# One index search over four key sets, with a second pass of the program kept as a fallback

## The chip, the cores and the metric

The kernel runs on one core of a Trainium2 chip. A core has five engines that follow their own instruction queues: PE (matrix products), DVE (vector work along the rows of 128 partitions), ACT (functions and scaled copies), POOL (here it issues the gathers) and SP (here it issues plain loads and stores). Results of PE lie in PSUM, all other tiles in SBUF. The metric is the device time of one execution in microseconds (us); the median of several runs counts.

## The reference

The output is the sum of three terms for 2048 tokens of 448 channels: the input `x`, a long causal convolution (part A), and a product-key mixture of experts (part B). The change is in part B, on the layer-normed input:

```python
q = einsum("nd,dhc->nhc", xf, w_q)            # 16 heads, two halves of 256
s1 = einsum("nhd,ed->nhe", q[..., :256], k1)  # 64 keys a half
s2 = einsum("nhd,ed->nhe", q[..., 256:], k2)
i1 = argsort(-s1)[..., :2]; t1 = the scores there     # the same for s2: i2, t2
cand = t1[..., :, None] + t2[..., None, :]            # 4 candidates
eidx = i1[..., :, None] * 64 + i2[..., None, :]
top_s, top_e = the best 2 of the 4 candidates, and their eidx
g = softmax(top_s)
act = gelu(einsum("nd,nhkd->nhk", xf, u[top_e]))
out = einsum("nhk,nhk,nhkd->nd", g, act, v[top_e])
```

So for each token, head and half, the two best of 64 scores are needed with their places; 32 such key sets a token. Two experts a head are 32 rows of `u` and `v` a token, fetched from HBM. Part A is a shift convolution, a product, a convolution of length 2048 by Fourier transforms, and a gate.

## The kernel before, in words

The 2048 tokens are 16 tiles T of 128 tokens. Three stages follow each other; within a stage the queues of all engines are filled by a planner.

**Weights.** `w_load` brings the query weights head by head, `w_keys` (L315) multiplies them by the keys on PE, `w_out` (L323) copies the product from PSUM on ACT, `w_turn` transposes it, and `w_high` and `w_low` (L339 to L347) split it into a high and a low part. The score of a key is then one product of a token with a column of 448 entries.

**Scores.** For each tile, `s_turn` (L359 to L364) transposes the tokens, `s_split` splits them, and `s_mm` (L375 to L379) makes 4 groups of 512 scores in one PSUM bank each: 8 key sets of 64 (4 heads of 2 halves), 11 products a group. `s_top` then works on DVE: for each set one MAX8 (L419), which writes the 8 largest of 64 scores, and one `max_index` (L417), which writes their 8 places. A `max_index` is two instructions, MATCH_VALUE_LOAD (the 8 values) and FIND_INDEX8 (the pass over the scores). `s_pairs` (L438 to L466) takes the first two values and places of each set for a pair of tiles, forms the candidates, their order and the expert numbers; `s_gate` forms the softmax of two on ACT; `s_place` (L498) and `s_put` (L481, L482) bring expert numbers and gates to the layout of the gathers, with ACT copies into `idx` (integers) and `gt`.

**Experts.** They run beside the scores and the convolution. `e_gather` (L520) issues 512 indirect DMAs from POOL, each with 128 rows of 3.5 KB; four make a block in one of four buffers `uv` (128 blocks in all). Per block, `e_dots` multiplies the `u` half by the tokens on DVE (L552 for several rows at once, L559 for one with its sum), `e_gelu` sums on ACT (L571) and takes the gelu (L575), `e_weigh` multiplies by the gates (L586) and, after the scores stage, spreads the weights on DVE (L591; `e_scale` does it on ACT, L601, in the scores stage), and `e_values` multiplies the `v` half on PE (L611, L614), which frees the buffer. `e_spread` (L533) copies tokens to the rows that need them, `e_fold` (L633, L635) adds the result to the output.

**Convolution.** It begins when the score buffers are freed: loads of `hkv` (L651), taps (L661 to L680), transforms (L705, L733, L765), products (L750 to L756), the way back (L781, L801) and the gate (L810, L815), in two halves of channels. The stores (L640) come last.

**The order.** Each function yields operations with an engine, a cost, what they wait for and which buffers they take. The planner keeps a clock per engine and picks, each time, the operation that could start first, or one of a lower priority number (`PRIO`) that starts soon enough. `HOP` is the time it allows for a wait across engines, `LATE` how long after the expected landing of a gather its product is placed, `BEHIND` how a gather is ordered behind PE instructions, `AHEAD` how far the convolution may run ahead of the gathers. In the scores stage, gathers come first while fewer than `LEAD` numbered gathers lie ready. The order is fixed when the kernel is built; an engine never departs from it.

Of the kernel before, what the change touches and what calls it, by code (L numbers as in the profile page):

```python
# [10 lines left out]
F32 = mybir.dt.float32  # L11
# [7 lines left out]
P = 128  # L19
# [8 lines left out]
BEHIND = 0.2  # L28
PAD = 1.0
LEAD = 12  # L30
SPAN, AHEAD, WORK = 25.0, -0.010, 548.0
# [47 lines left out]
PRIO = {"c_back": 0.5, "c_delta": -0.1, "c_fin": -0.1, "c_fm": -0.4, "c_gate": -0.1, "c_hh": 0.4, "c_in": 0.5, "c_inv": 0.2, "c_load": -0.4, "c_mul": -0.2, "c_prod": 0.1, "c_spec": 0.3, "c_store": 0.2, "c_tap": 0.5, "c_turn": 0.4, "c_zt": 0.3, "e_dots": 0.2, "e_fold": -0.3, "e_gather": -0.2, "e_gelu": -0.2, "e_out": -0.1, "e_scale": -0.3, "e_spots": -0.2, "e_spread": -0.5, "e_values": -0.5, "s_gate": 0.1, "s_put": -0.5, "s_split": 0.1, "s_top": 0.3, "s_turn": 0.1}  # L79
# [18 lines left out]
class Planner:  # L98
# [3 lines left out]
    HOP, SLIP, RATE = 0.70, 1.20, 0.35  # L102
# [89 lines left out]
def parallel_kernel(ctx, tc, x, wq, kk, uv, hkv, const, fq, out):  # L192
    nc = tc.nc
    ctx.enter_context(tc.manual_schedule())
    ap = ctx.enter_context(tc.tile_pool(name="ap", bufs=1))
# [36 lines left out]
    xls = [wp.tile([P, KC + 1, P], F32R, name=f"xl{i}") for i in range(2)]  # L232
    live = {}
# [165 lines left out]
    def s_top(groups):  # L399
        for group in groups:  # L400
            n_t = len(group)
            def begin(n_t=n_t):
                live["mx"] = wp.tile([P, 2, 32, 8], F32, tag="mx", name="mx")
                live["mi"] = wp.tile([P, 2, 32, 8], U32, tag="mi", name="mi")

            for i, T in enumerate(group):
                for n in range(4):
                    for what in range(2):
                        for j0 in range(0, 8, 2):
                            def top(i=i, T=T, n=n, j0=j0, what=what, begin=begin):  # L410
                                if T % 2 == n == j0 == what == 0:
                                    begin()
                                mx, mi, sc = live["mx"], live["mi"], live["sc", T, n]
                                for j in range(j0, j0 + 2):
                                    m = mx[:, T % 2, 8 * n + j, :]
                                    if what:
                                        nc.vector.max_index(mi[:, T % 2, 8 * n + j, :], m, sc[:, 64 * j:64 * j + 64])  # L417
# [495 lines left out]
```

## Time and profile before

| What | Value |
| --- | --- |
| Median of 3 runs | 825.22 us (823.52 to 825.5) |
| The profiled execution's own time | 829.65 us |
| Span of its profile | 827.8 us |
| Busy in the span: PE, DVE, ACT, POOL | 675.5, 695.4, 560.2, 492.6 us |
| FIND_INDEX8 of L417 | 512 of 225 ns on the mean |
| MATCH_VALUE_LOAD of L417 | 512 of 75 ns |
| MAX8 of L419 | 512 of 217 ns |
| Gathers of L520 | 512, 234.91 MB, 77.0% of the DMA engines' time |
| All DMA | 278.53 MB, 336 GB/s over the span |

The profile follows one execution. A group is all instructions of one line, engine and shape; "mean ns" is the length of one from start to end, and as an engine begins an instruction before the one ahead has ended, 512 times the mean can be more than the time that they take. "Idle before" is how long the engine stood still in front of the group's instructions, with what ended it. The chain of work that ended last is followed back from the last instruction. A table of stretches gives each engine's busy time in a window of the span, with the granted clock of PE, the busy share of the DMA engines and what they moved.

### The profile page before, as it was taken

The numbers are of one execution on the slowest core, as the hardware profiler recorded it, in microseconds if no ns is written. First come the engines' busy times: TensorE is split into PE (matmuls) and PEld (weight loads), VectorE is DVE, ScalarE is ACT, GpSimd is POOL, SyncE is SP. The second block draws the span as 40 slices with busy tenths as digits, with TensorE's granted clock in tenths as the row PEclk, the third lists the DMA queues.
The fourth block names the chain that finished last, engine by engine and source line by source line (L and its number), as shares of the span: only waits on it lengthen the run. The fifth ranks groups of instructions, "written<-read, shape, count | busy, mean of one in ns | idle before, by whom it ended". The sixth has DMA issues, their size and how long they took to land.

```text
span 827.8 us, 16797 instructions
## 1 busy us (share of the span) xinstructions
PE 675.5 (82%) x5052; PEld 392.6 (47%) x5052; DVE 695.4 (84%) x2600; ACT 560.2 (68%) x1926; POOL 492.6 (60%) x518
## 2 busy tenths in 40 slices
PE   6994799999999989846776879787867778878784
PEld 2463456566565556414543344335545543433461
DVE  3369698999999999964898999996859989999674
ACT  4458997677777768664785765766557857666752
POOL 0004666666666757764577666667564776777770
PEclk9998699999998999956987989999888999999897
DMA  9954898999988989999999899999999999999995
GB/s 331 381 210 171 304 337 312 324 338 335 326 316 312 339 286 344 353 341 377 363 320 322 307 400 331 399 340 371 379 383 322 332 378 396 385 399 378 347 379 191
DMA packets 80555, 278.53 MB, mean 336 GB/s; under 512 B 10321, under 2 KB 47569, under 8 KB 80465
## 3 DMA queue, kind: packets, MB, share of 16 engines
q0 software_dynamic: 40960, 234.91, 77.0%
q1 hardware_dynamic: 39360, 42.41, 15.2%
q8 instruction: 41, 0.67, 0.3%
q14 instruction: 50, 0.40, 0.1%
q10 hardware_dynamic: 144, 0.13, 0.1%
HBM read 273.75 MB, written 3.67 MB: 335 GB/s over the span
## 4 chain that ended last, share of the span: by engine, by line
DVE 49%; DMA 20%; PE 17%; ACT 5%; issue 4%; SPq 4%; POOL 1%; DVEq 0%; POOLq 0%; ACTq 0%
DVE uv L552 18%; DMA uv<-in_uv_dram,idx 12%; DVE mi L417 9%; DMA x<-in_hkv_dram 7%; DVE mx L419 6%; SPq L651 4%; PE pw L315 4%; ACT uv L571 3%; PE pv L614 2%; PE psu L765 2%; DVE tap L672 2%; DVE tap L670 2%; DVE hh L751 2%; DVE hh L750 2%; DVE hh L755 2%
## 5 line engine op out<-in xcount | busy, mean ns | idle before, releaser
L520 POOL DMA_INDIRECT uv<-in_uv_dram,idx x512 | 491.9, 961 | 315.7 <-issue 94.0
L571 ACT ACTIVATE uv<-uv 128x448 f32<-128x448 f32 x457 | 257.7, 565 | 108.7 <-DVE uv L552 106.7
L552 DVE TENSOR_TENSOR uv<-xr,uv 128x1792 f32<-128x1792 f32 (+3 forms) x128 | 232.4, 1817 | 34.1 <-DMA uv<-in_uv_dram,idx 29.6
L614 PE MATMUL pv<-uv,cc 128*32 128x448 f32 x1024 | 144.9, 606 | 0.0
L417 DVE FIND_INDEX8 mi<-mx,sc 128x8 uint32<-128x64 f32 x512 | 104.1, 225 | 0.0
L765 PE MATMUL psu<-hh,fm 128*128 128x224 f32 x264 | 69.4, 388 | 25.8 <-DVE hh L756 16.7
L571 ACT ACTIVATION_READ_ACCUMULATOR uv<-uv 128x1 f32 x457 | 85.6, 187 | 0.0
L375 PE MATMUL sc<-wh,xh 128*128 128x512 f32 x192 | 81.9, 426 | 4.2 <-DVE mi L417 2.7
L705 PE MATMUL ps<-cst,x 128*64 128x132 f32 x896 | 69.2, 315 | 18.7 <-DVE x L687 6.5
L765 PEld LDWEIGHTS psu<-hh,fm 128*128 128x128 f32 x264 | 48.0, 200 | 71.0 <-ACT uv L571 43.0
L705 PEld LDWEIGHTS ps<-cst,x 128*64 128x64 f32 x896 | 60.4, 158 | 41.6 <-issue 20.4
L419 DVE MAX8 mx<-sc 128x8 f32<-128x64 f32 x512 | 74.3, 217 | 5.3 <-PE sc L379 5.2
L377 PE MATMUL sc<-wh,xl 128*128 128x512 f32 x192 | 77.0, 401 | 0.0
L376 PE MATMUL sc<-wl,xh 128*128 128x512 f32 x192 | 76.8, 400 | 0.0
L733 PE MATMUL psf<-x,fm 128*128 128x448 f32 x132 | 64.3, 575 | 2.5 <-DMA fm<-in_fq_dram 0.7
L611 PE MATMUL pv<-uv,cc 128*1 128x4 bf16 x128 | 21.6, 169 | 51.9 <-DVE cc L591 41.2
L611 PEld LDWEIGHTS <-cc 128*1 128x1 bf16 x128 | 10.2, 80 | 107.4 <-DVE cc L591 64.3
L601 ACT ACTIVATE cc<-rep,w 128x32 f32<-128x32 f32 x200 | 47.4, 308 | 9.6 <-DVE w L586 9.6
L375 PEld LDWEIGHTS sc<-wh,xh 128*128 128x128 f32 x192 | 36.9, 192 | 35.3 <-issue 14.8
L533 PE MATMUL xr<-xn,rep 32*128 32x448 f32 x128 | 34.8, 620 | 13.8 <-DVE uv L552 10.7
L715 ACT ACTIVATE x<-ps 128x396 f32<-128x396 f32 (+1 forms) x84 | 35.4, 457 | 14.4 <-PE ps L705 14.4
L624 ACT ACTIVATE vs<-pv 128x448 f32<-128x448 f32 x64 | 34.1, 532 | 13.2 <-PE pv L614 12.9
(103 smaller groups left out, 1036.8 us busy)
## 6 DMA issues: line engine op xcount, KB each, us to landing
wq<-in_wq_dram SPq DMA_DIRECT2D x16, 896.0 KB
x<-in_hkv_dram SPq DMA_DIRECT2D x14, 780.0 KB
fm<-in_fq_dram SPq DMA_DIRECT2D x66, 128.0 KB
uv<-in_uv_dram,idx POOLq DMA_INDIRECT x512
out_dram<-acc SPq DMA_DIRECT2D x32, 112.0 KB
acc<-in_x_dram SPq DMA_DIRECT2D x1, 2240.0 KB
acc<-in_x_dram SPq DMA_DIRECT2D x1, 896.0 KB
cst<-in_const_dram SPq DMA_DIRECT2D x1, 540.0 KB
```

The source lines that it names most:

```text
L375: nc.tensor.matmul(sc, xh[:, c, :], wh[:, c, ns], start=(c == 0), stop=False)
L376: nc.tensor.matmul(sc, xh[:, c, :], wl[:, c, ns], start=False, stop=False)
L377: nc.tensor.matmul(sc, xl[:, c, :], wh[:, c, ns], start=False, stop=False)
L417: nc.vector.max_index(mi[:, T % 2, 8 * n + j, :], m, sc[:, 64 * j:64 * j + 64])
L419: nc.vector.max(m, sc[:, 64 * j:64 * j + 64])
L520: made = nc.gpsimd.indirect_dma_start(live["uv", b][:, c, :], None, uv, bass.IndirectOffsetOnAxis(ap=idx[:, T, g:g + 1], axis=0)).ins
L552: nc.vector.tensor_mul(u, live["xr", T, j][:, None, :D].broadcast_to([P, na, D]), u)
L571: nc.scalar.activation(u, u, AF.Copy, accum_out=live["act", b][:, c:c + 1])
L614: nc.tensor.matmul(pv[32 * c:32 * c + 32, :D], cc[:, c, :], buf[:, c, D:], start=(hf == 0), stop=(hf == 1), tile_position=(0, 32 * c))
L705: nc.tensor.matmul(ps[64 * i:64 * i + 64, w * j:w * j + w], src, f1[:, i, :], start=True, stop=True, tile_position=(0, 64 * i))
L733: nc.tensor.matmul(ps[:, :2 * HALF], live["fm", g, q][:, 0], x1[:, :, :, q, :].rearrange("p c t k -> p t c k"), start=True, stop=True)
L765: nc.tensor.matmul(ps[:, :HALF], fm[:, 1], hh[:, i], start=(i == 0), stop=(i == 1))
```

## The change

Four key sets (two heads of two halves, 256 neighbouring scores in one PSUM bank) share one `max_index`. Its 8 needles are the two best of each of the four sets. For that, MAX8 of set g writes its 8 values at places 2g to 2g+7 of a row of `mx`; the next one overwrites all but the first two. So that a value of one set isn't met in an earlier one, the columns of set i of four are scaled by 32 to the power i while the weights are copied (`w_out`), and the maxima are scaled back in `s_pairs`.

The places come back counted within 256. `second` subtracts 64 i + 31.5, so that each lies between -31.5 and 31.5 in its own set, and keeps the largest distance; `third` limits the expert numbers to the table, and `s_put` adds the offset again. `first` keeps the largest score. After the scores stage, `s_stray` brings the worst distance and score of all tokens to one number (a small DVE reduction, one PE transpose, another reduction) and writes a flag. At the end of the program all engines load the flag, and only if it is set they run the program a second time, with one `max_index` a set as before.

The number of MAX8 stays at 512; `max_index` falls from 512 over 64 scores to 128 over 256. Five constants of the planner and the table of priorities have other values.

```diff
-BEHIND = 0.2
+STEP, HIGHEST = 32.0, 1e30
+BEHIND = 0.5
-SPAN, AHEAD, WORK = 25.0, -0.010, 548.0
+SPAN, AHEAD, WORK = 25.0, -0.030, 548.0
...
-    HOP, SLIP, RATE = 0.70, 1.20, 0.35
+    HOP, SLIP, RATE = 0.20, 1.20, 0.35
...
+    stray = fp.tile([1, 1], I32, name="stray")
+    program(tc, *args, stray)
+    found = nc.values_load(stray, min_val=0, max_val=1)
+    with tc.If(found > 0):
+        program(tc, *args, None)
...
+        for i in range(4):
+            nc.vector.memset(base[:, i], 64.0 * i + MID)
+            nc.vector.memset(up[64 * (i % 2):64 * (i % 2) + 64, i // 2:i // 2 + 1], STEP ** i if stray is not None else 1.0)
+            nc.vector.memset(down[:, i:i + 1], STEP ** -i)
+        nc.vector.memset(far, 0.0)
+        nc.vector.memset(top_s, 0.0)
+        nc.vector.memset(mid, 65 * MID)
...
-                nc.scalar.activation(live["ws", h], live.pop(("pw", h))[:, :D], AF.Copy)
+                nc.scalar.activation(live["ws", h], live.pop(("pw", h))[:, :D], AF.Copy, scale=up[:, h % 2:h % 2 + 1])
...
-                live["mx"] = wp.tile([P, 2, 32, 8], F32, tag="mx", name="mx")
-                live["mi"] = wp.tile([P, 2, 32, 8], U32, tag="mi", name="mi")
+                live["mx"] = wp.tile([P, 136], F32, tag="mx", name="mx")
+                live["mi"] = wp.tile([P, 2, 64] if stray is not None else [P, 2, 32, 8], U32, tag="mi", name="mi")
...
+                                if what and stray is not None:
+                                    g = 2 * (8 * n + j0)
+                                    nc.vector.max_index(mi[:, g:g + 8], mx[:, g:g + 8], sc[:, 64 * j0:64 * j0 + 256])
+                                    return
                                 for j in range(j0, j0 + 2):
-                                    m = mx[:, T % 2, 8 * n + j, :]
+                                    g = 8 * n + j
+                                    m = mx[:, 2 * g:2 * g + 8]
...
+            if stray is not None:
+                m8 = live["mx"][:, 64 * (T0 % 2):64 * (T0 % 2 + n_t)].rearrange("p (s g e) -> p s g e", g=4, e=2)
+                nc.vector.tensor_mul(m8, m8, down[:, None, :, None].broadcast_to([P, 8 * n_t, 4, 2]))
+                nc.vector.tensor_reduce(top_s[:, T0:T0 + 1], m8.rearrange("p s g e -> p (s g e)"), op=ALU.max, axis=mybir.AxisListType.X, apply_absolute_value=True)
...
+                rel = wp.tile([P, 8 * n_t, 4, 2], F32, tag="rel", name="rel", padded_shape=[P, 16, 4, 2])
+                nc.vector.tensor_sub(rel, live["mi"][:, part].rearrange("p a (s g e) -> p (a s) g e", g=4, e=2), base[:, None].broadcast_to([P, 8 * n_t, 4, 2]))
+                nc.vector.tensor_reduce(far[:, T0:T0 + 1], rel.rearrange("p s g e -> p (s g e)"), op=ALU.max, axis=mybir.AxisListType.X, apply_absolute_value=True)
...
-            nc.vector.tensor_add(es[:, :, :, 1], e01, e2[:, :, :, 1])
-            nc.vector.tensor_copy(es[:, :, :, 0], e2[:, :, :, 0])
+            nc.vector.tensor_add(e2[:, :, :, 1], e01, e2[:, :, :, 1])
+            nc.vector.tensor_scalar(es, e2, -65 * MID, 4095 - 65 * MID, op0=ALU.max, op1=ALU.min)
...
-                nc.scalar.activation(idx[:, T].rearrange("p (j k) -> p j k", k=8), pe[:, :, 0], AF.Copy)
+                nc.scalar.activation(idx[:, T].rearrange("p (j k) -> p j k", k=8), pe[:, :, 0], AF.Identity, bias=mid)
...
-    LATE = 0.5
+    LATE = 2.0
...
+    def s_stray():
+        def worst():
+            live["ls"] = ap.tile([P, 1], F32, name="ls")
+
+            nc.vector.scalar_tensor_tensor(far, top_s, 1e3 / HIGHEST, far, op0=ALU.mult, op1=ALU.max)
+            nc.vector.tensor_reduce(live["ls"], far, op=ALU.max, axis=mybir.AxisListType.X)
+        yield Op("DVE", 0.4, worst, key=("ls",))
...
+    if stray is not None:
+        plan.run([plan.add(0, s_stray())])
```

More of the change, by code (lines that the diff above doesn't have):

```diff
@@ L232, in parallel_kernel @@
     xls = [wp.tile([P, KC + 1, P], F32R, name=f"xl{i}") for i in range(2)]
+    base = ap.tile([P, 4, 2], F32, name="base")
+    far, top_s = (ap.tile([P, NT], F32, name=name) for name in ("far", "top_s"))
+    mid = ap.tile([P, 1], F32, name="mid")
+    MID = 0.0 if stray is None else 31.5
+    up, down = (ap.tile([P, n], F32, name=name) for n, name in ((2, "up"), (4, "down")))
     live = {}
@@ L408, in s_top @@
                     for what in range(2):
-                        for j0 in range(0, 8, 2):
+                        for j0 in range(0, 8, 4 if what and stray is not None else 2):
                             def top(i=i, T=T, n=n, j0=j0, what=what, begin=begin):
@@ L457, in second @@
             nc.vector.scalar_tensor_tensor(e01, i4[:, :, 0, 0], 64.0, i4[:, :, 1, 1], op0=ALU.mult, op1=ALU.add)
-        yield Op("DVE", 0.55, second)
+        yield Op("DVE", 0.55 if stray is None else 1.1, second)
         def third():
@@ L850, in parallel_kernel, with turn, put @@
     plan.show("scores")
+    def s_stray():
[4 more added lines that the diff above has]
+        yield Op("DVE", 0.4, worst, key=("ls",))
+        def turn():
+            live["pl"] = ps_a.tile([P, 512], F32, tag="a", name="pl")
+            nc.tensor.transpose(live["pl"][:1, :P], live["ls"], ident)
+        yield Op("PE", 0.3, turn, [("ls",)], key=("pls",), rings=[(r_a, ("stray",))], lag=0.2)
+        def put():
+            one = ap.tile([1, 1], F32, name="one")
+            nc.vector.tensor_reduce(one, live["pl"][:1, :P], op=ALU.max, axis=mybir.AxisListType.X)
+            nc.vector.tensor_scalar(stray, one, 32.0, None, op0=ALU.is_gt)
+        yield Op("DVE", 0.4, put, [("pls",)], key=("stray",))
+    if stray is not None:
+        plan.run([plan.add(0, s_stray())])
     ws_ctx.close()
```

25 lines of the change are left out of this document (16 added, 9 removed).

## The prediction

> **What bounds the kernel now.** The page comes first: the span and the engines' shares. Then the table of stretches, since the program has three stages: weights (to about 57 us), scores with gathers (to about 357 us), convolution with gathers (to the end).
>
> ```profile
> span 827.8 us, 16797 instructions
> DVE uv L552 18%; DMA uv<-in_uv_dram,idx 12%; DVE mi L417 9%; DMA x<-in_hkv_dram 7%; DVE mx L419 6%; SPq L651 4%; PE pw L315 4%; ACT uv L571 3%; PE pv L614 2%; PE psu L765 2%; DVE tap L672 2%; DVE tap L670 2%; DVE hh L751 2%; DVE hh L750 2%; DVE hh L755 2%
> ```
>
> ```profile
> core 0: us, PE busy (x) PEld busy (x) DVE busy (x) ACT busy (x) POOL busy (x), PEclk, DMA share, GB/s
> 160.00:200.00 40.00, 39.75 (x239) 23.91 (x238) 39.83 (x242) 30.17 (x116) 26.84 (x30) 1.00 0.92 325
> 360.00:400.00 40.00, 26.00 (x205) 15.24 (x199) 20.90 (x46) 23.39 (x88) 18.98 (x20) 0.63 1.02 358
> 520.00:560.00 40.00, 32.42 (x153) 15.91 (x151) 36.80 (x75) 26.51 (x93) 26.90 (x29) 0.91 0.98 368
> 680.00:720.00 40.00, 32.76 (x167) 15.67 (x166) 38.22 (x76) 28.13 (x96) 28.07 (x31) 1.00 1.02 391
> ```
>
> In the scores stage DVE is busy 39.83 of 40 us, and the find L417 is 9% of the chain that ended last. PE looks as full (39.75), while the DMA engines move 325 GB/s, less than the 391 of a later stretch. In the convolution DVE is again the fullest engine (36.80 and 38.22 of 40), but for a hole at 360 us, where the first loads come in. So DVE binds twice, and the change takes DVE work out of the first stage. The groups of 120:357, the steady part of that stage, give the parts:
>
> ```profile
> L552 DVE TENSOR_TENSOR uv<-xr,uv 128x1792 f32<-128x1792 f32 x42 | 84.5, 2014 | 2.7 <-DMA uv<-in_uv_dram,idx 2.4 <-issue 0.3
> L417 DVE FIND_INDEX8 mi<-mx,sc 128x8 uint32<-128x64 f32 x410 | 83.5, 226 | 0.0
> L419 DVE MAX8 mx<-sc 128x8 f32<-128x64 f32 x408 | 59.4, 218 | 0.6 <-PE sc L379 0.6
> L375 PE MATMUL sc<-wh,xh 128*128 128x512 f32 x152 | 64.7, 425 | 4.2 <-DVE mi L417 2.7 <-DVE mx L419 1.4
> L378 PE MATMUL sc<-wr,xh 128*128 128x512 f32 x51 | 20.2, 396 | 0.0
> L359 PE MATMUL px<-ident,xn 128*128 128x128 f32 (+1 forms) x88 | 14.1, 291 | 0.5 <-DVE mi L417 0.5
> L533 PE MATMUL xr<-xn,rep 32*128 32x448 f32 x44 | 11.3, 589 | 4.2 <-DVE uv L552 4.2
> L498 PE MATMUL pe<-eg,ident 128*32 128x32 f32 x192 | 4.0, 237 | 0.0
> ```
>
> DVE has hardly any idle time in front of these groups. In these 237 us stand 410 finds, the products L552 of 42 gather blocks (four gathers each, so 5.64 us a block), and 3 x 152 + 2 x 51 = 558 score matmuls (L376 and L377 run as often as L375, L379 as L378).
>
> **The finds.** Neighbouring rows of the timeline give start-to-start times, which are what a full engine pays (durations overlap):
>
> ```profile
> 340.21 0.17 PE L611 MATMUL pv<-uv,cc 128*1 128x4 bf16 x1
> 340.22 0.95 PE L614 MATMUL pv<-uv,cc 128*32 128x448 f32 x8
> 340.29 1.13 DVE L419 MAX8 mx<-sc 128x8 f32<-128x64 f32 x8
> 340.49 0.95 POOL L520 DMA_INDIRECT uv<-in_uv_dram,idx  x1 [0.30 <-issue]
> 341.34 0.07 DVE L417 MATCH_VALUE_LOAD mi<-mx,sc 128x8 f32 x1
> 341.40 0.22 DVE L417 FIND_INDEX8 mi<-mx,sc 128x8 uint32<-128x64 f32 x1
> 341.54 0.07 DVE L417 MATCH_VALUE_LOAD mi<-mx,sc 128x8 f32 x1
> 341.74 0.95 POOL L520 DMA_INDIRECT uv<-in_uv_dram,idx  x1 [0.30 <-issue]
> 342.13 0.39 PE L376 MATMUL sc<-wl,xh 128*128 128x512 f32 x1
> 342.36 0.39 PE L377 MATMUL sc<-wh,xl 128*128 128x512 f32 x1
> ```
>
> A find (its value load included) takes 341.54 - 341.34 = 0.20 us, eight maxima (341.34 - 340.29) / 8 = 0.13 us each, a score matmul 0.23 us, a gather 1.25 us on POOL. A find over 256 elements isn't in the trace. Elements cost as follows:
>
> ```profile
> L552 DVE TENSOR_TENSOR uv<-xr,uv 128x1344 f32<-128x1344 f32 x25 | 38.8, 1552 | 8.1 <-DMA uv<-in_uv_dram,idx 7.9
> L591 DVE TENSOR_TENSOR cc<-rep,w 128x128 f32<-128x128 f32 x78 | 22.9, 294 | 4.4 <-PE ps L705 0.5
> L248 DVE TENSOR_REDUCE rep<-ident 128x32 f32<-128x128 f32 x4 | 1.2, 360 | 0.5 <-POOL ident masks.py:199 0.5
> L456 DVE SCALAR_TENSOR_TENSOR e<-mi 128x64 f32<-128x64 uint32 x7 | 1.5, 217 | 0.0
> ```
>
> From 1344 to 1792 elements L552 grows by 462 ns: 1.03 ns an element. So 192 more elements add 0.20 us, and I take 0.40 us a find. The ends are 0.20 (elements free) and 0.60 (two cycles an element, which would be 132 of the 226 ns of today's find); 1.03 ns is the nearest row. The 410 finds of 0.20 us are 82 us; 410 / 4 = 102.5 of 0.40 us are 41. **41 us go** (21 to 61).
>
> **What comes in on DVE.** Per pair of tiles: a product and a difference over 128 elements (0.29 each, L591), two reductions (0.36 each, L248), and a clamp for a copy (about nothing); with four waits of a few hundredths, 1.4 us, about 9 us for the 6.4 pairs of this stretch. The check at the end is seven small instructions, some 1 us, beside other work. The constants are 15 small memsets at the start, under the first weight load, which lands at 7.77:
>
> ```profile
> 1.24 6.53 DMA wq<-in_wq_dram
> ```
>
>  Without that cover they would be about 1 us. On ACT the scaled copy and the bias stand where plain copies stood: nothing (ACT is busy 30.17 of 40 us, so its slack covers it). Tile 1's maxima now come behind tile 0's last find, an order that the in-order DVE has already. So **DVE falls by about 31 us** in the 237.
>
> **What then is late.** PE. Its own score work is 558 x 0.23 = 128 us plus 18 us (L359, L498), 146 in all; each block adds 0.95 (L614), 0.17 (L611) and 11.3 / 42 = 0.27, so 1.4 us. That is 146 + 59 = 205 of 237 us, 86%. DVE keeps 237 - 31 = 206 us of work for the same blocks: both engines come to the same size. At blocks of 5.64 us, with PE filled to 95%, the stage lasts 146 / (0.95 - 1.4 / 5.64) = 208 us and holds 37 blocks; at POOL's best of 5.0 us a block 146 / (0.95 - 0.28) = 218 us and 44. So the stage ends 29 or 19 us sooner, and leaves the convolution 5 blocks more or 2 less. There a block costs DVE:
>
> ```profile
> L552 DVE TENSOR_TENSOR uv<-xr,uv 128x1792 f32<-128x1792 f32 (+3 forms) x79 | 133.8, 1694 | 29.7 <-DMA uv<-in_uv_dram,idx 25.9 <-PE xr L533 3.0 <-issue 0.2
> L559 DVE SCALAR_TENSOR_TENSOR uv<-xr,uv 128x448 f32<-128x448 f32 x55 | 33.3, 617 | 1.1 <-DMA uv<-in_uv_dram,idx 0.9
> ```
>
> These and L591 are 190 us for about 77 blocks, 2.5 each, 2.7 with the small products, 2.9 at DVE's 92% there. So 15 us come back in the one case and 6 go in the other: 14 to 25 net. I take **19**. (Bounds: 0 if PE's busy time is real. By DVE alone, at 2.1 us a block with its small products, 206 - 42 x 2.1 = 118 us of score work take 118 / (1 - 2.1 / 5.0) = 203 us: 34 less, with 41 blocks.)
>
> [...]
>
> **The end.** After the last store every engine loads the flag and jumps over a second program as long as the first. Nothing like it is in the trace.
>
> ```profile
> 806.72 6.23 DMA uv<-in_uv_dram,idx
> 819.85 5.43 SPq L640 DMA_DIRECT2D out_dram<-acc  x11
> 820.79 0.62 DVE L635 TENSOR_TENSOR acc<-pf,acc 128x448 f32<-128x448 f32 x1 [3.42 <-PE pf L633]
> ```
>
> Below: 0 us, if the jump lies inside the 2.5 us between the last issue (819.85 + 5.43 = 825.28) and the end of the span; the other engines jump earlier, and nothing but the end is queued behind the flag. Above: 12 us, two rounds of a DMA under load (6.23 for the gather). I take 5, a DMA on an idle queue (2.5) and as much again for flag and barrier. Compare-and-branch is given as about 108 ns in the Trainium skill (Advanced Engine Details and Errata, Control Flow Timing); by that alone the sum would be 5 lower. No run here shows it; the skill also says (Runtime: NRT & Kernel Launch, Instruction fetch mechanics) that a jump out of the fetched pages waits for a fetch.
>
> **The new constants** change the order everywhere. LATE = 2.0 puts the products further behind their gathers; DVE waits 25.9 us for gathers in the convolution (row above). I take 3 of these as saved; ends: 20 saved, 10 lost.
>
> **The sum** stands against the profiled execution's own 829.65 us (span 827.8, 1.85 around it): 829.65 - 19 + 5 - 3 = 812.65. The median of the runs shown is 825.22, 4.4 lower, so the forecast is **808 us**.
>
> **Rivals.**
> 1. PE is no bound. DVE alone gives a stage 34 us shorter, with one block (+4, rounded up) left for later; the jump is hidden and LATE saves 15: 829.65 - 34 + 4 - 15 - 4.4 = 780. For it: PEld's 60%. Against: PE has waits of its own in the stage (L375, L533, 4.2 us each). Range 770 to 795, chance 0.15.
> 2. All is given back. The stage ends 25 us sooner at the old pace of gathers, 18 gathers stay over, and the convolution is paced by its gathers: +26, as the row of its gathers gives (297.8 + 151.5) / 307 = 1.46 us each.
>
> ```profile
> L520 POOL DMA_INDIRECT uv<-in_uv_dram,idx x307 | 297.8, 970 | 151.5 <-issue 59.0 <-PE ps L705 14.3 <-ACT uv L571 13.1
> ```
>
>    With 5 for the end: 829.65 - 25 + 26 + 5 - 4.4 = 831; 822 to 832. For it: a DMA share of 1.02 in the row of 680:720. Against: that row carries 391 GB/s, more than the convolution's other rows. Chance 0.13.
> 3. Slower: the maxima serialise. Each MAX8 now writes eight places of which the next overwrites six. Rows with a dependence show what a wait costs:
>
> ```profile
> 356.85 0.21 DVE L438 TENSOR_TENSOR best<-mx 128x64 f32<-128x64 f32 x1
> 356.97 0.21 DVE L439 TENSOR_TENSOR other<-mx 128x32 f32<-128x32 f32 x1
> 357.22 0.19 DVE L440 TENSOR_TENSOR dd<-best,other 128x32 f32<-128x32 f32 x1
> ```
>
> Independent neighbours start 0.12 us apart; L440, which reads its predecessor's output, starts 0.04 after that one's end. A MAX8 that waits so takes 0.22 + 0.03 = 0.25 us instead of 0.13, 408 x 0.12 = 49 us more: DVE +18 in the stage, 18 / (1 - 2.1 / 5.64) = 29 with the gathers that go on meanwhile, and 5 for the end: 829.65 + 34 - 4.4 = 859. It decides above 0.13 + 31 / 408 = 0.21 us a maximum. Against: both are writes in order, and no row shows writes waiting for writes. Chance 0.08.
> 4. The check trips and the second program runs: about 1,630 us. The scales of 32 keep the four sets' best apart. Chance 0.02.
>
> **The numbers.** Forecast 0.62, from 796 to 820. A measurement of this kernel tells about 0.3% (2.5 us) from no change: faster is below 822.7, slower above 827.7. Rival 2 gives 0.01 to faster, 0.06 to the same, 0.06 to slower. Faster 0.78, same 0.06, slower 0.16. The range 787 to 832 holds the forecast, rival 2 and half of rival 1.
>
> **What would show it.** The 256-element find at 0.40 us, MAX8 still at 0.13; the last find near 333 us instead of 357; PE's waits in the stage smaller and DVE's larger; 200 gathers or so by then; the time from the last DVE instruction to the end some 5 us longer. A find above 0.60 us or a MAX8 above 0.21 us would break the sum, as would a convolution stage that grows by as much as the first shrinks.

## The result, and the profile after

The changed kernel takes 853.53 us (median of 4 runs, 851.61 to 859.13) where the kernel before takes 825.06 (median of 4): a ratio of 1.036, with a 95% interval from 1.031 to 1.041. It is slower, by 28 us, where 808 us had been forecast. The profiled execution took 859.13 us.

The span comes first, with the lines of the chain of work that ended last.

```profile
span 857.3 us, 16111 instructions
DVE uv L598 18%; DVE mx L455 10%; DMA x<-in_hkv_dram 8%; DMA uv<-in_uv_dram,idx 8%; DVE mi L447 4%; SPq L697 3%; ACT uv L617 3%; PE pw L345 3%; PE pv L660 3%; PE psf L779 2%; DMA fm<-in_fq_dram 2%; DVE tap L718 2%; DVE hh L801 1%; DVE hh L797 1%; DVE hh L796 1%
```

The share of the find (`mi`) in the chain that ended last went from 9% to 4%, as it should. The share of the maxima (`mx`), which nobody meant to touch, went from 6% to 10%.

The same stretches of the span as before (us busy of PE, PEld, DVE, ACT and POOL, each with its number of instructions; clock; DMA share; GB/s):

```profile
160.00:200.00 40.00, 36.82 (x221) 23.06 (x219) 37.79 (x127) 29.86 (x113) 24.65 (x26) 1.00 0.89 306
360.00:400.00 40.00, 22.36 (x173) 9.92 (x171) 24.86 (x67) 23.29 (x85) 22.66 (x24) 0.70 0.97 350
520.00:560.00 40.00, 31.30 (x159) 14.80 (x160) 38.23 (x74) 27.42 (x97) 26.48 (x28) 1.00 1.02 393
680.00:720.00 40.00, 31.35 (x184) 15.64 (x181) 35.43 (x81) 23.48 (x79) 24.24 (x27) 0.96 0.93 331
```

In the scores stage DVE runs 127 instructions in 40 us where it ran 242, and is still busy for 37.79 of them. PE makes 221 products where it made 239, and POOL issues 26 gathers where it issued 30. So the stage has fewer DVE instructions and yet is no faster. The timeline of DVE says why (start, length, line, operation):

```profile
200.60 2.08 DVE L455 MAX8 mx<-sc 128x8 f32<-128x64 f32 x8
202.60 0.07 DVE L447 MATCH_VALUE_LOAD mi<-mx,sc 128x8 f32 x1
202.66 0.42 DVE L447 FIND_INDEX8 mi<-mx,sc 128x8 uint32<-128x256 f32 x1
...
207.40 0.07 DVE L447 MATCH_VALUE_LOAD mi<-mx,sc 128x8 f32 x1
207.46 0.42 DVE L447 FIND_INDEX8 mi<-mx,sc 128x8 uint32<-128x256 f32 x1
207.80 0.07 DVE L447 MATCH_VALUE_LOAD mi<-mx,sc 128x8 f32 x1
```

A find over 256 takes 207.80 - 207.40 = 0.40 us, the forecast figure. But eight maxima take 202.60 - 200.60 = 2.00 us, 0.25 each on the mean; before they took 0.13 each. The groups of the stretch 120:366 show how easily that is missed:

```profile
L455 DVE MAX8 mx<-sc 128x8 f32<-128x64 f32 x400 | 92.3, 231 | 12.9 <-PE sc L409 1.0
L598 DVE TENSOR_TENSOR uv<-xr,uv 128x1792 f32<-128x1792 f32 x42 | 84.7, 2016 | 0.0
L405 PE MATMUL sc<-wh,xh 128*128 128x512 f32 x147 | 63.1, 429 | 0.0
```

One MAX8 lasts 231 ns from start to end, against 218 before. What differs is the busy time: 92.3 us / 400 is those whole 231 ns, where before 59.4 / 408 was 146. Before, each one began while its predecessor was still finishing; now none does, and DVE stands idle for 12.9 / 400 = 32 ns besides.

The span falls into three parts: up to the last find, from there to the last DVE instruction (the convolution), and the tail. For the changed kernel (called after from here on), the rows that bound them (last find, last stores, last DVE instruction):

```profile
365.62 0.42 DVE L447 FIND_INDEX8 mi<-mx,sc 128x8 uint32<-128x256 f32 x1
...
840.21 11.54 SPq L686 DMA_DIRECT2D out_dram<-acc  x17
...
845.07 0.62 DVE L681 TENSOR_TENSOR acc<-pf,acc 128x448 f32<-128x448 f32 x1 [4.18 <-PE pf L679]
```

| us | last find | convolution | tail | span |
| --- | --- | --- | --- | --- |
| before | 356.7 | 464.7 | 6.4 | 827.8 |
| after | 365.6 | 480.1 | 11.6 | 857.3 |
| difference | +8.9 | +15.4 | +5.2 | +29.5 |

The parts are those of the two profiled executions, each 4 to 6 us above the median of its kernel (829.65 against 825.06, 859.13 against 853.53).

The gathers are not what differs. By the last find 204 were issued before and 203 after (of 512; one that lies on the border counts in both parts):

```profile
0.00:356.70 356.70, 193.12 (x204) 0.95 0.88 314
356.70:827.00 470.30, 298.79 (x308) 0.89 0.96 354
```

```profile
0.00:365.60 365.60, 191.74 (x203) 0.95 0.87 304
365.60:857.00 491.40, 300.14 (x310) 0.90 0.94 341
```

(Columns: POOL busy with the gathers and their count, clock, DMA share, GB/s; first before, then after.)

### The profile page after: what moved, and what is told of

It is laid out like the page before. It is cut to its first block, busy times and chain, and to the rows that moved or that the text cites. A ratio compares the mean times of both kernels' runs of the same rounds, so it can differ in the third digit from the quotient of the medians.

```text
span 857.3 us, 16111 instructions
## 1 busy us (share of the span) xinstructions
PE 674.7 (79%) x5053; PEld 392.4 (46%) x5053; DVE 699.4 (82%) x1887; ACT 561.9 (66%) x1926; POOL 492.6 (57%) x518
## 4 chain that ended last, share of the span: by engine, by line
DVE 46%; DMA 19%; PE 18%; issue 5%; ACT 5%; SPq 3%; POOL 1%; DVEq 0%; POOLq 0%; ACTq 0%
DVE uv L598 18%; DVE mx L455 10%; DMA x<-in_hkv_dram 8%; DMA uv<-in_uv_dram,idx 8%; DVE mi L447 4%; SPq L697 3%; ACT uv L617 3%; PE pw L345 3%; PE pv L660 3%; PE psf L779 2%; DMA fm<-in_fq_dram 2%; DVE tap L718 2%; DVE hh L801 1%; DVE hh L797 1%; DVE hh L796 1%
## 5 line engine op out<-in xcount | busy, mean ns | idle before, releaser
L455 DVE MAX8 mx<-sc 128x8 f32<-128x64 f32 x512 | 118.1, 231 | 22.5 <-PE sc L409 7.2
L779 PE MATMUL psf<-x,fm 128*128 128x448 f32 x132 | 66.3, 588 | 31.2 <-DMA fm<-in_fq_dram 11.0
L405 PE MATMUL sc<-wh,xh 128*128 128x512 f32 x192 | 82.4, 429 | 0.0
L407 PE MATMUL sc<-wh,xl 128*128 128x512 f32 x192 | 76.3, 397 | 0.0
L811 PE MATMUL psu<-hh,fm 128*128 128x224 f32 x264 | 64.5, 369 | 6.1 <-ACT uv L617 2.1
L447 DVE FIND_INDEX8 mi<-mx,sc 128x8 uint32<-128x256 f32 x128 | 52.7, 423 | 0.0
L405 PEld LDWEIGHTS sc<-wh,xh 128*128 128x128 f32 x192 | 37.2, 194 | 30.5 <-issue 17.4
L779 PEld LDWEIGHTS psf<-x,fm 128*128 128x128 f32 x132 | 21.0, 192 | 62.0 <-ACT uv L617 19.4
```

The lines of the kernel that those rows point to most:

```text
L405: nc.tensor.matmul(sc, xh[:, c, :], wh[:, c, ns], start=(c == 0), stop=False)
L407: nc.tensor.matmul(sc, xl[:, c, :], wh[:, c, ns], start=False, stop=False)
L447: nc.vector.max_index(mi[:, g:g + 8], mx[:, g:g + 8], sc[:, 64 * j0:64 * j0 + 256])
L455: nc.vector.max(m, sc[:, 64 * j:64 * j + 64])
L779: nc.tensor.matmul(ps[:, :2 * HALF], live["fm", g, q][:, 0], x1[:, :, :, q, :].rearrange("p c t k -> p t c k"), start=True, stop=True)
L811: nc.tensor.matmul(ps[:, :HALF], fm[:, 1], hh[:, i], start=(i == 0), stop=(i == 1))
```

## The experiments

**Theories.** The main one: each MAX8 waits for the end of the one whose places it overwrites, 512 x 0.12 = 61 us of DVE work, which eats what the shared find saves. Its rivals: the jump over the second program; the new constants of the planner; and the shared find itself, if the 256-wide find or the operations around it cost more than priced.

The places of the main theory are in the built program. The queue of DVE reads, for one group of 8 sets, before:

```
L419 Max mx<-sc 128x8 [waits PE_49]
L419 Max mx<-sc 128x8 x7
L417 MaxIndex mi<-mx,sc 128x8 [waits DVE_49] x8
```

and after:

```
L455 Max mx<-sc 128x8 [waits PE_49]
L455 Max mx<-sc 128x8 [waits DVE_49] x7
L447 MaxIndex mi<-mx,sc 128x8
L447 MaxIndex mi<-mx,sc 128x8 [waits DVE_49]
```

(The number in brackets is the semaphore's.) Seven of eight maxima now wait on DVE's own semaphore, for the write that they partly cover.

### First group, on a chip where the kernel before takes 824.10 us

**e1_two_chains**: the shared find stays, and the overwriting too, but the maxima of the two finds of a group alternate between two tiles, so that each covers the places of the one before last (the product that scales back then writes a compact tile, which the later steps read).

```diff
-live["mx"] = wp.tile([P, 136], F32, tag="mx", name="mx")
+live["mx"] = wp.tile([P, 2, 8, 16], F32, tag="mx", name="mx")
...
-for j in range(j0, j0 + 2):
+for j in (j0 // 2, j0 // 2 + 4):
     g = 8 * n + j
-    m = mx[:, 2 * g:2 * g + 8]
+    m = mx[:, 2 * n + j // 4, 2 * (j % 4):2 * (j % 4) + 8]
...
```

> The change with the eight-place writes of MAX8 in two chains: the four sets of one find still overlap each other, but the two finds of a group have places of their own (16 apart), and the maxima of the two chains alternate, so that each overlaps only with the one before the last. Everything else is as in the change, the second pass and the new constants too. Theory W (a MAX8 that overwrites its predecessor's places waits for that one to end, 0.25 us instead of 0.13): eight maxima take about 1.05 us again instead of 2.0, DVE loses 61 us over the run, the last find comes near 335 us instead of 366, and the time falls by 30 to 45 us, to 810 to 824. Theory O (the new constants and the order made from them cost the time): MAX8 may be faster, but the end stays at 845 or above, since the convolution keeps its length.

Measured: 818.95 us, ratio 0.9953 [0.9912, 0.9994], 10 runs from 813.65 to 832.55. The maxima, in the timeline of e1:

```profile
200.47 1.15 DVE L455 MAX8 mx<-sc 128x8 f32<-128x64 f32 x8
201.53 0.08 DVE L447 MATCH_VALUE_LOAD mi<-mx,sc 128x8 f32 x1
201.60 0.42 DVE L447 FIND_INDEX8 mi<-mx,sc 128x8 uint32<-128x256 f32 x1
```

(201.53 - 200.47) / 8 = 0.13 us: the pace of before is back. Six of eight still carry a wait on DVE's own semaphore, but for the one before last, which is over by then. So it is not the wait as an instruction that costs, but waiting for the direct predecessor's end. Some 34 of the 45 us between forecast and result (853.53 - 808) go with it: (1.036 - 0.9953) x 825, within 5 by the two intervals. With the maxima at 0.13 the last find starts at 325.3 us, 31 earlier than before (19 to 29 had been forecast; f1 below, with the constants of before, comes to 22). And PE becomes the full engine, in the stretches and in the chain of e1:

```profile
120.00:160.00 40.00, 40.00 (x255) 25.04 (x254) 37.81 (x147) 34.10 (x130) 29.42 (x32) 1.00 0.98 365
160.00:200.00 40.00, 40.00 (x277) 24.56 (x273) 37.79 (x147) 33.37 (x129) 29.91 (x33) 1.00 0.98 358
200.00:240.00 40.00, 40.00 (x244) 25.03 (x241) 37.42 (x141) 33.35 (x126) 30.25 (x33) 1.00 0.99 371
```

```profile
PE 36%; DVE 25%; DMA 23%; ACT 6%; SPq 4%; issue 3%; POOL 1%; DVEq 0%; POOLq 0%; ACTq 0%
DMA uv<-in_uv_dram,idx 11%; DVE uv L601 10%; DMA x<-in_hkv_dram 8%; PE pv L663 6%; PE sc L405 5%; ACT uv L620 4%; DMA fm<-in_fq_dram 4%; PE sc L406 4%; PE sc L407 4%; SPq L700 4%; PE pw L345 3%; PE psf L782 2%; PE px L389 2%; DVE mx L455 2%; DVE tap L721 2%
```

The score products L405 to L407 stand in this chain, and DVE's maxima are down to 2%. In 160:200 every piece of the chain is PE's. POOL is at its pace too (32 to 33 gathers in 40 us, at 1.25 each); it has 1% of the chain, but no run frees the one engine and not the other.

**e2_overlap_alone**: the kernel before with little but the overwriting: the program in its second form (512 finds over 64, maxima two places apart; the clamp stays, and the scaled copy with scale 1), once, with the constants of before (their lines are left out below; they are those of the next group).

```diff
...
-    program(tc, *args, stray)
-    found = nc.values_load(stray, min_val=0, max_val=1)
-    with tc.If(found > 0):
-        program(tc, *args, None)
+    program(tc, *args, None)
```

> The kernel before, with only the overlapping places of MAX8: 512 finds over 64 scores each, no scaling, no check of places, no second pass, the constants of before. Theory W: MAX8 takes 0.25 us each, DVE has 61 us more work, 50 of it in the steady scores stage; this stage was full, so it grows by 30 to 75 us, and the time is 850 to 890. Theory O: MAX8's places cost nothing worth naming, 825 to 832.

Measured: 887.94 us, ratio 1.0726 [1.0659, 1.0792]. Its scores stretch:

```profile
160.00:200.00 40.00, 31.37 (x189) 18.73 (x188) 37.38 (x202) 22.61 (x85) 21.72 (x23) 0.96 0.79 263
...
202.46 1.02 DVE L451 MAX8 mx<-sc 128x8 f32<-128x64 f32 x4
203.41 0.07 DVE L449 MATCH_VALUE_LOAD mi<-mx,sc 128x8 f32 x1
```

Four maxima take 0.95 us, 0.24 each, and there are 189 products where there were 239. The last find comes at 418.1 us instead of 356.7: 61.4 later, as much as 512 x 0.12 (56 at the 0.11 of this row), with the same 204 gathers issued by then and a convolution of 464.9 us (464.7 before). So in this stage of the kernel before an us of DVE work is an us of time.

**e3_no_second**: the change without the load of the flag and without the second program (the flag is still made).

> The change without the flag's load, the branch and the second pass (the check still computes its flag, which nobody reads). If the time from the last DVE instruction to the end is the price of the branch, it falls from 11.6 us to the 6.4 of before, and the time falls by 5 us, to 848 or 849. If the branch was hidden, it stays at 853.

Measured: 848.33 us, ratio 1.0255 [1.0198, 1.0312]. That is 5 us below the change by the medians and 9 by the ratios, whose intervals just touch. The profile is clearer: the tail is 6.8 us instead of 11.6, so the jump costs its forecast 5 us. It is not the cause of the miss.

**e4_before_new_consts**: the kernel before with BEHIND, AHEAD, HOP, LATE and PRIO of the change (four numbers, not five, and the table).

> The kernel before with the change's constants and priorities alone (BEHIND, AHEAD, HOP, LATE, PRIO). Theory W has no part in it: if the constants are harmless, 820 to 828. Theory O: the convolution stage is 12 us longer as in the change, 835 to 842 or more.

Measured: 841.95 us, ratio 1.0202 [1.013, 1.0274]. In the kernel before, the constants alone cost 17 us. They pull gathers forward (229 instead of 204 by the last find), which then comes 15.8 us later (POOL busy with the gathers and their count, clock, DMA share, GB/s):

```profile
0.00:372.50 372.50, 216.44 (x229) 0.95 0.91 331
372.50:841.00 468.50, 275.40 (x284) 0.88 0.91 331
```

The convolution has 24 gathers fewer to serve and is only 3 us shorter. The expectation had a convolution 12 us longer in its theory O; the total of that theory (835 to 842) came out, but from another stage. Whether the constants cost the change as much is the next groups' question.

### Second and third group: the constants

The second group came to a chip on which the kernel before takes 912.16 us, and differences there turned out smaller; the third came to one like the first (823.91). The same edits are set side by side; ratios are to the kernel before on the same chip.

**e5_chains_old_consts** and **f1_chains_old_consts** are e1 with the constants of before; **e6** and **f2** are the same without the second program; **e7** and **f3** are the change with the constants of before; **e8_before_prio** is the kernel before with only the new PRIO, **f4_before_rest** with only the other four numbers.

```diff
-BEHIND = 0.5
+BEHIND = 0.2
...
-SPAN, AHEAD, WORK = 25.0, -0.030, 548.0
+SPAN, AHEAD, WORK = 25.0, -0.010, 548.0
...
-    HOP, SLIP, RATE = 0.20, 1.20, 0.35
+    HOP, SLIP, RATE = 0.70, 1.20, 0.35
...
-    LATE = 2.0
+    LATE = 0.5
```

(PRIO goes back as well in e5 to e7 and f1 to f3; f4 is this diff the other way round, in the kernel before.)

> The change with the two chains of maxima and the constants and priorities of before. If the slow maxima and the new constants are the two causes, and add up, it wins over the two chains alone what these constants cost the kernel before (17 us): the last find at about 325 us again, the convolution and the end together about 475 us, 800 to 806. If the constants suit the change and hurt only the old kernel, it is no faster than the two chains alone: 815 to 830.

> The same without the flag's load, the branch and the second pass (the check still computes its flag, which nobody reads). The end costs 5 us, as in the change: 795 to 801, 5 below its sister. If the price of the end was hidden or came from elsewhere, the two are equal.

> The change with the constants and priorities of before, its maxima still overlapping. If the constants cost the change what they cost the kernel before, 836 to 842; if the slow maxima are the whole cause and the constants hurt only the old kernel, 850 to 856.

> The kernel before with the table of priorities of the change alone. All new constants together cost it 17 us. If the table (s_place, s_put and the convolution's steps in another order) carries that, 836 to 844; if it is LATE, HOP, AHEAD or BEHIND, 822 to 830.

> The change with the two chains of maxima and the constants of before, again, since the kernel before took 912 us on the chip of the last call and 824 on that of the first. If the slow maxima and the constants are two causes that add up: 800 to 806 beside a kernel before of 820 to 826, that is 2 to 3% faster. If the constants suit the change, it is no faster than the two chains alone (0.5% faster than before).

> The same without the flag's load, the branch and the second pass. If the end costs 5 us here too: 795 to 801, and the time from the last DVE instruction to the end back at 6.4 us.

> The change with the constants of before, its maxima still overlapping. If the constants cost the change what they cost the kernel before (17 us): 836 to 842, so that maxima and end alone make it 1.5 to 2% slower than before. If only the maxima matter: 850 to 856.

> The kernel before with LATE, HOP, AHEAD and BEHIND of the change, but its own priorities: the other half of the new constants, whose sum cost 17 us. If the priorities carry most of it (they cost 11 us on the chip of the last call), this is 826 to 832; if these four carry it, 836 to 842.

| kernel | second group | third group |
| --- | --- | --- |
| e1's chains, constants of before | e5: 915.60 us, 1.0025 [0.9992, 1.0058] | f1: 828.90 us, 1.0068 [1.0033, 1.0102] |
| the same, no second program | e6: 908.73, 0.9953 [0.9933, 0.9973] | f2: 825.70, 1.0026 [0.9996, 1.0056] |
| the change, constants of before | e7: 924.06, 1.0135 [1.0083, 1.0186] | f3: 863.34, 1.0477 [1.0414, 1.0539] |
| before, new PRIO | e8: 923.41, 1.0107 [1.0054, 1.0161] | |
| before, the four numbers | | f4: 833.76, 1.0108 [1.0041, 1.0175] |

PRIO alone and the four numbers alone each cost the kernel before 1.1%, together 2.0% (e4). But on the chips where the kernel before takes 824 us the constants help the shared find by 1.2% (1.0477 to 1.036 in the change, 1.0068 to 0.9953 with two chains). So their effect has a sign of its own in each kernel: the expectations of 800 to 806 us for f1 and of 856 at most for f3, which took the constants for harmful or harmless, both failed. On the other chips no gain is seen (0.9953 in e6 without the constants, 0.9983 and 0.9961 in g1 and h1 below with them). One thing that they do for the shared find can be read in the waits of DVE for gathers (total, times, longest; first f1, then e1, whose only difference they are):

```profile
DVE uv L601 <- DMA uv<-in_uv_dram,idx: 35.4, 30, 3.3
```

```profile
DVE uv L601 <- DMA uv<-in_uv_dram,idx: 9.2, 8, 4.3
```

f1 and f2 left another question: with the maxima at 0.13 us and the constants of before, the last find comes 22 us sooner (334.4 us), and yet the kernel is no faster than before. The parts of the spans, in single profiled executions (before's took 4.4 us more than the median, e1's 5.3 less than its own):

| us | last find | gathers issued after it | convolution | tail |
| --- | --- | --- | --- | --- |
| before | 356.7 | 308 | 464.7 | 6.4 |
| e1 | 325.3 | 312 | 475.4 | 11.2 |
| f1 | 334.4 | 317 | 478.6 | 11.4 |
| f2 | 332.7 | 317 | 483.4 | 6.3 |
| e3 | 369.1 | 310 | 475.0 | 6.8 |
| f3 | 366.8 | 316 | 483.0 | 11.6 |

Every kernel with the shared find has a convolution that is 10 to 19 us longer, early or late. It has 2 to 9 gathers more to serve, but these do not measure the loss: after has 2 more and lost 15.4 us, f1 has 9 more and lost 13.9. By the prediction's 2.9 us a block, 9 gathers are 6.5 us. One difference lies at the turn between the two halves of channels. The `hkv` loads of the second half take longer to be issued, as each waits for its buffer (before, then e1):

```profile
563.66 47.02 SPq L651 DMA_DIRECT2D x<-in_hkv_dram  x7
```

```profile
540.40 58.70 SPq L700 DMA_DIRECT2D x<-in_hkv_dram  x7
```

and the products L733 behind them (L782 in e1), with the taps' spectrum, are fewer in a stretch of 30 us that begins 300 us after the last find: 18 before, 8 in e1 (PE, PEld busy; clock; DMA share; GB/s; before, then e1):

```profile
656.70:686.70 30.00, 8.12 (x18) 3.26 (x18) 1.00 0.99 370
```

```profile
625.30:655.30 30.00, 3.78 (x8) 1.27 (x8) 0.89 0.94 317
```

In f1, however, those loads take 42.8 us, less than before, and its products are only 4 in that stretch. So the late loads alone do not explain the loss.

The convolution, as counted here, begins and ends with an instruction of DVE, so DVE's own time says more. It is busy there for 384.3 us before, 387.9 in e1, 388.1 in after and 390.2 in f1: 4 to 6 us more, about what the blocks left over cost. The rest is idle time. One wait is longer in all six kernels with the shared find on such chips than in before and in e2: that of the taps for the `hkv` loads, 24.8 us before and 25.9 in e2, but 29.8 in f1, 31.9 in e1, 34.4 in f2, 36.2 in after, 36.8 in e3 and 37.0 in f3. That is 5 to 12 of the 10 to 19 us. The new constants lengthen it in the kernel before as well (32.8 in e4). Why the loads come later is not shown.

### Fourth and fifth group: what lengthens the convolution

Both came to chips like that of the second group (before: 904.95 and 905.29 us).

**g1_chains_no_second**, again as **h1_chains_no_second**: e1 without the second program. **g2_chains_hold**: e1, with SP held ahead of the convolution until block 52 has landed, so as to start it with more gathers done. **g3_chains_half_rows**, again as **h2_chains_half_rows**, and **g4_before_half_rows**: from block 51 on each gather brings rows of half the length.

```diff
+    plan.run([plan.add(0, [Op("SP", 0.0, lambda: None, [("land", 52, 3)])])])
     ws_ctx.close()
```

```diff
-made = nc.gpsimd.indirect_dma_start(live["uv", b][:, c, :], None, uv, ...
+made = nc.gpsimd.indirect_dma_start(live["uv", b][:, c, :] if b < 51 else live["uv", b][:, c, :D], None, uv if b < 51 else uv.rearrange("n (w d) -> (n w) d", w=2), ...
...
-    nc.tensor.matmul(pv[32 * c:32 * c + 32, :D], cc[:, c, :], buf[:, c, D:],
+    nc.tensor.matmul(pv[32 * c:32 * c + 32, :D], cc[:, c, :], buf[:, c, D:] if b < 51 else buf[:, c, :D],
...
```

The half rows come from other rows, and the second product reads the same half as the first: these kernels run the instructions of the others, but leave out half of the experts' data.

> The change with the two chains of maxima and its own constants, without the flag's load, the branch and the second pass. The end costs 5 us, the maxima 34: 812 to 816 beside a kernel before of 824, 1 to 1.5% faster. If the convolution is paced by the gathers and takes the 5 us back, 817 to 821.

> The two chains with the convolution held back in the order until block 52 has landed, so that more of the gathers are issued ahead of it (some 212 to 220 instead of 201). Theory G (the convolution is paced by the gathers left, about 1.5 us each): the convolution shortens by 1.5 us for each gather fewer, from 475 us to 450 to 460, and the time stays within 6 us of the two chains alone (819). The other theory (the convolution's length is set by its own order and work): it stays at 470 or more, and the time grows by the 10 to 20 us of the hold.

> The two chains, but from block 51 on a gather brings rows of 1792 bytes instead of 3584 (only a first half, of other rows; the second product reads that half too), so that the convolution's gathers move half the bytes with the same instructions. If the bytes pace the convolution (DMA share 0.96), it falls from 475 us to 400 to 430. If DVE and the order pace it, it stays above 455.

> The kernel before with the same halved rows from block 51 on. If its convolution (465 us) is paced by bytes too, it falls to 390 to 425; if it is paced by DVE and the order and only the change's is paced by bytes, it stays above 450 while that of the change comes down to the same length.

> The two chains without the second pass, again, since the kernel before took 905 us on the chip of the last call. Beside a kernel before of 824: 812 to 816 if the 5 us of the end come on top, 1 to 1.5% faster; on a chip where the kernel before takes over 900 us, the same as before again.

> The two chains with rows of 1792 bytes from block 51 on (a first half, of other rows; the second product reads that half too), again, on this call's chip. If bytes pace the convolution where the kernel before takes 824 us, it falls from 475 us to 400 to 430. If only its order and the engines do, as on the last chip (507 after 523), it stays above 455.

| kernel | us | ratio |
| --- | --- | --- |
| g1, h1 | 903.47, 902.16 | 0.9983 [0.9961, 1.0005], 0.9961 [0.9937, 0.9984] |
| g2 | 920.07 | 1.0169 [1.0122, 1.0216] |
| g3, h2 | 894.59, 891.70 | 0.9890 [0.9854, 0.9927], 0.9856 [0.9817, 0.9895] |
| g4 | 890.97 | 0.9859 [0.9799, 0.9920] |

g2 did not do what it was made for: 201 gathers were issued by the last find, as without the hold, so it does not bear on the question. The half rows do. The convolution of g3 and of g4 (PE, PEld, DVE, ACT, POOL, clock, DMA share, GB/s):

```profile
375.30:882.30 507.00, 379.19 (x3226) 206.94 (x3226) 389.88 (x786) 304.07 (x1026) 302.69 (x312) 0.91 0.66 190
```

```profile
391.70:886.60 494.90, 382.96 (x3218) 208.95 (x3216) 384.17 (x774) 300.84 (x1016) 299.25 (x308) 0.90 0.66 189
```

With the DMA engines at 0.66 of their time instead of 0.9 or more, the convolution with the shared find is still 12 us longer than that of before (507.0 against 494.9), and against g1 (522.8 us) only 16 us of it have gone. So on these chips the bytes are not what lengthens it. What does, the runs do not settle, and on a chip of 824 us it was not tried.

## Why the prediction was wrong

**The step that failed.** The prediction listed what comes in on DVE (four operations, a clamp, memsets) and left the maxima at their old 0.13 us, since "both are writes in order, and no row shows writes waiting for writes". The rows of after show it: 0.25 us. This was its third rival, given 0.08, and 0.25 lies above its own decision point of 0.21. Its price per maximum, 0.22 for the length and 0.03 for the start after the predecessor's end, is met in part by luck: of its rows only L440 depends on its predecessor, and it starts 0.04 after that one's end. So it is here: a maximum that waits starts (2.08 - 0.23) / 7 = 0.26 us after its predecessor. The mean of eight is 0.25, as the value load follows the last of them sooner. The trace of before could not show such a wait, because there each MAX8 had places of its own. The diff could: `2 * g:2 * g + 8` covers six places of the predecessor, and the program orders such writes with the semaphore that it uses for reads. Whether the chip would keep the order without the wait wasn't tried.

The Trainium skill (VectorE: DVE Perf Modes, The DRAIN you can't avoid) reports eight copies on DVE that took the same time with a semaphore after each as with one at the end. For MAX8 the trace here differs: 1.06 us for eight that do not wait for their direct predecessor, 2.00 for eight of which seven do.

**The finds**: right. 0.40 us for 256 elements, so 51 of the 102 us of all 512 finds go.

**The added operations**: right. In the groups of after (the whole span, pairs of tiles):

```profile
L476 DVE TENSOR_TENSOR mx<-mx,down 128x128 f32<-128x128 f32 x7 | 2.0, 290 | 0.2
L477 DVE TENSOR_REDUCE top_s<-mx 128x1 f32<-128x128 f32 x7 | 2.0, 286 | 0.2
L497 DVE TENSOR_TENSOR rel<-mi,base 128x128 f32<-128x128 uint32 x7 | 2.0, 281 | 0.0
L498 DVE TENSOR_REDUCE far<-rel 128x1 f32<-128x128 f32 x7 | 2.0, 286 | 0.2
```

290, 286, 281 and 286 ns, against 290 and 360 taken: 8 us in all, with a few tenths each for the tiles that come singly.

**DVE's balance in the scores**, over all 512 maxima and finds, is then +61 - 51 + 9 = +19. (The prediction's -31 and the third rival's +18 count the 410 of the steady part.) The stage grew by 8.9 us (10.1 in f3, which has the constants of before and 8 gathers fewer in the stage). Up to the last find DVE is busy for 311.1 us before and 311.3 after, and idle for 45.6 and 54.3. The idle time in front of the maxima rose by 17 us (5.3 to 22.5), all other idle time fell by some 8: half of the extra work went where DVE had been waiting for others.

**The factor of the third rival**, 1/(1 - 2.1/5.64), took the gathers to go on at their pace while DVE is late. They don't: e2's stage grew by the bare 61 us with the 204 gathers of before, since the built order fixes what stands ahead of what. The rival's 859 us lies near 853.5 only because the 20 us that it put too much into the stage (29 against 8.9) are nearly what the convolution gave back (15.4).

**PE becomes the bound**: borne out once the maxima are free (e1), with 325.3 us for the last find, though POOL is as full and the two were not told apart. The Trainium skill (Perfetto Trace Analysis, Identifying the Most-Contended Engine) judges PE's headroom by the share of its peak rate and by weight-load busy time, not by matmul busy time. In e1 weight loads stand at 25 of 40 us while the whole chain of 160:200 is on PE, so here weight-load time alone would not have pointed at PE; the start-to-start time did.

That the forecast for a profiled execution, 812.65 us, lies beside e1's 813.65 is in part luck. The stage gave 31 us instead of 19 to 29, the convolution took back 11 for one block more, and of the two executions compared that of before took 4.4 us more than its median and that of e1 5.3 less. By the medians e1 gains 5 us where 17 had been forecast.

**The step from profiled execution to median**, 4.4 us lower, did not hold for e1: its profiled execution is the fastest of its ten, 5.3 us below their median of 818.95. Of the miss of 45 us, 34 are the overlap; the other 11 stand between 808 and e1, and this step makes up nearly all of them.

**The blocks left over**: e1's 4 gathers more are one block, 3 us by the prediction's price. Its convolution is 10.7 us longer. The prediction named a convolution that grows as a sign against it, but had it priced by blocks alone. The price fits DVE's busy time there (3.6 us more); the other 7 us are idle time, as much as the wait for `hkv` grew (24.8 to 31.9), whose cause stays open.

**The end**: right, 5 us (11.6 against 6.4 in the tail; 6.8 without the second program). The Trainium skill gives some 108 ns for a compare-and-branch (Advanced Engine Details and Errata, Control Flow Timing); no row here shows the branch by itself.

**The constants**, forecast at -3 (from -20 to +10): -10 in the changed kernel (1.2%), +17 in the kernel before. They had been priced by one wait alone, LATE against the gathers. That wait did fall, by 7 us from f3 to after, whose only difference they are; the waits of the taps for `hkv` stayed, and those for the gelu of ACT rose from 8.8 to 16.3 us. Together these three do not give the 10 us, whose source stays open (first f3, then after; total, times, longest):

```profile
DVE x L733 <- DMA x<-in_hkv_dram: 37.0, 6, 10.5
DVE uv L598 <- DMA uv<-in_uv_dram,idx: 19.4, 14, 4.1
```

```profile
DVE x L733 <- DMA x<-in_hkv_dram: 36.2, 11, 7.7
DVE uv L598 <- DMA uv<-in_uv_dram,idx: 12.0, 8, 3.1
```

**The best version** is e1: 818.95 us, 0.5% under the kernel before, with an interval that ends just below 1: hardly to be told from no change. Without the second program it ran only on the chips of the last two groups (0.998 and 0.996).

## What to carry to other kernels

When an edit lets a short instruction write where its predecessor has just written, price it from start to end and not from start to start. Here the difference was half of its time (0.13 against 0.25 us), and the mean length of its group (218 against 231 ns) hardly showed it. Give such a chain a second tile and alternate; here that brought the 0.12 us back. And hold constants of a planner apart from the change when it is priced: here the same numbers were worth -1.2% in one kernel and +2% in the other.

## What the runs showed of the hardware

- MAX8 over 64 elements: 0.13 us from start to start when it waits for nothing or for the one before last; 0.26 when it waits for its direct predecessor, 0.25 on the mean of eight with seven such waits.
- A find and its value load take 0.20 us over 64 elements and 0.40 over 256.
- Loading a flag and jumping over a second program as long as the first: 5 us at the end of the kernel (tails of 11.6 and 11.4 us in after and f1, of 6.8 and 6.3 in e3 and f2).
- Chips differ. f1 took 828.9 us on one, the same kernel as e5 915.6 on another, at nearly the same granted clock (0.922 and 0.911 in the profiled executions). In e5's profile PE and ACT stand idle with nothing seen that releases them, as in these rows of its waits (total, times, longest):

```profile
PEld psu L814 <- issue: 53.7, 39, 7.2
...
ACT uv L620 <- issue: 27.6, 22, 5.4
```

All such waits of PEld together are some 268 us in e5 and 112 in f1. What they wait for isn't shown. A saving on one engine is worth less there: the change with the constants of before costs 4.8% on the one and 1.4% on the other.
